# Fusing the stages of a transducer joint's forward and backward pass into one stream of 512-column chunks

## The chip, the cores and the metric

The kernel runs on one core of a Trainium2 chip. The metric is device time of that core in microseconds (us): the median of several runs of one kernel. The profiles are taken from one of those runs, so a span in a profile differs a little from a median.

Engines in the profile: PE is the matmul engine (TensorE), PEld its weight loads, DVE is VectorE, ACT is ScalarE, POOL is GpSimd, SP is SyncE. "PEclk" is the granted clock of TensorE as a share of full speed. In these kernels PSUM is where matmuls leave their sums, SBUF where the other tiles lie, and DRAM holds inputs, outputs and spills (data stored and loaded again later). Some traces lack matmul records (7790 matmuls for 7868 weight loads in the kernel before), so PE's busy time is probably a few us too small.

## The reference

Two convolutions of width 3 and stride 2 with a tanh-approximated gelu, then a joint of every time step with every one of 8 labels, then the gradients of all seven inputs. With B=2, T=16000, D=V=256 the joint has 4000 time steps per batch. The core of it:

```python
h = einsum over 3 taps of x with w1;   h = gelu(h)[:, ::2, :]     # (2, 8000, 256)
f = einsum over 3 taps of h with w2;   f = gelu(f)[:, ::2, :]     # (2, 4000, 256)
fe = f @ w_f;   ge = g @ w_g                                      # g: (2, 8, 256)
j = tanh(fe[:, :, None, :] + ge[:, None, :, :])                   # (2, 4000, 8, 256)
out = j @ w_o
_out, _vjp = jax.vjp(_f, x, w1, w2, g, w_f, w_g, w_o)
_grads = _vjp(grad_out)        # the outputs are out and the seven gradients
```

(The first five lines are shortened; the padding is left out.) Everything is bfloat16 in memory, with FP32 sums.

## The kernel before

Each batch passes through five stages, one after the other. Each stage has its own buffers, above all its own PSUM pools, which are freed before the next begins. A batch has 8 chunks of 512 columns (a column is a time step; the last chunk has 416), and every stage goes over all of them.

1. Conv: both convolutions and their gelu. The gelu derivatives and a row-major copy of h go to DRAM.
2. Joint: tanh, outputs, the gradient through tanh, the sum of it over the labels, the gradient of w_o.
3. GF/GH: gradients back through w_f, gelu, w2, gelu.
4. W2/WF: weight gradients, with transposes on PE and copies of them.
5. x/W1: the gradient of x (tile GX_SB, stored straight to DRAM) and of w1.

The gelu, which sets the pace of the conv stage: four operations on VectorE and ScalarE lie between the matmuls and the release of their PSUM buffer, then five more make the derivative.

```python
def gelu_from_psum(wk, Pps, W, h_out, gp_out):
    sq = wk.tile([P, KT, CW], BF16, name="g_sq")
    nc.scalar.activation(out=sq[:, :, :W], in_=Pps, func=ACT.Square, scale=GELU_SQRT_K)
    inner = wk.tile([P, KT, CW], BF16, name="g_inner")
    nc.vector.scalar_tensor_tensor(out=inner[:, :, :W], in0=sq[:, :, :W], scalar=1.0, in1=Pps,
                                   op0=ALU.add, op1=ALU.mult)
    s = wk.tile([P, KT, CW], BF16, name="g_s")
    nc.scalar.activation(out=s[:, :, :W], in_=inner[:, :, :W], func=ACT.Sigmoid, scale=GELU_A)
    nc.vector.tensor_tensor(out=h_out, in0=s[:, :, :W], in1=Pps, op=ALU.mult)
    # ... five more operations for the derivative gp_out (one on ScalarE, four on VectorE)
```

The order of stages, and what is spilled between them:

```python
for b in range(B):
    # ... GE = g @ w_g
    with tc.tile_pool(name="psA", bufs=2, space=PSUM) as psA, ...:      # stage 1
        for ci in range(n_cchunks + 1):
            if ci < n_cchunks:
                conv1_chunk(ci, wk, g1p, psA)      # ends in a store of both derivatives to G1D
            if ci >= 1:
                conv2_chunk(ci - 1, wk, g2p, psB)  # ends in a store to G2D
                hrc_chunk(ci - 1, hrp, psHR)       # transposes of h, stored to HRD
    # ... stage 2, joint, over all chunks
    # ... stage 3: d1_chunk / d5_chunk, reload G2D and G1D
    # ... stage 4: reload HRD; per 256 columns:
            pe_transpose8(psD3t, FNg[:], srcs)     # 8 transposes and one copy of 1024 columns
            pe_transpose8(psD3t, GFR[:], srcs)
            # ... matmuls into GWF_ps and GW2_ps, which stay in PSUM for the whole batch
    # ... stage 5: GX_SB and GW1_ps, which stays in PSUM too
```

Of the kernel before, what the change touches and what calls it, by code (L numbers as in the profile page):

```python
# [10 lines left out]
BF16 = mybir.dt.bfloat16  # L11
# [10 lines left out]
def kernel(  # L22
# [31 lines left out]
    n_cchunks = (MQ + CW - 1) // CW  # L54
    MQ_PAD = n_cchunks * CW
    NBLK = MQ_PAD // 128
    CBLK = CW // 128
    HOFF = 16
    HW = HOFF + MQ_PAD + 16
    GFW = MQ_PAD + 128  # L60
    TBF = 512
    assert TBF <= CW and MQ_PAD % TBF == 0
    NTB = TBF // 128
    n_tb_total = MQ_PAD // 128
    n_jchunks = MQ_PAD // TBF

    const = ctx.enter_context(tc.tile_pool(name="const", bufs=1))
    accp = ctx.enter_context(tc.tile_pool(name="accp", bufs=1))
    dram = ctx.enter_context(tc.tile_pool(name="dscr", bufs=1, space=bass.MemoryType.DRAM))

    xcp = ctx.enter_context(tc.tile_pool(name="xc", bufs=3))
    xq = x.rearrange("b (q four) d -> b four q d", four=4)

    def load_xc(bb, ci):
        mc0 = ci * CW
        W = min(CW, MQ - mc0)
        XC = xcp.tile([P, 4, KT, CW + 16], BF16, name="XC")
        if ci == 0:
            nc.vector.memset(XC[:, :, :, 0:16], 0.0)
            q0, j0, n = 0, 16, W  # L80
        else:
            q0, j0, n = mc0 - 16, 0, W + 16
        for c in range(4):
            nc.sync.dma_start_transpose(out=XC[:, c, :, j0:j0 + n], in_=xq[bb, c, q0:q0 + n, :])
        return XC

    xc_prefetched = {(0, 0): load_xc(0, 0)}

    ident = const.tile([P, P], BF16, name="ident")
    make_identity(nc, ident[:])  # L90
    ones = const.tile([P, 8], BF16, name="ones")
    nc.vector.memset(ones[:], 1.0)
    biasA = const.tile([P, 1], FP32, name="biasA")
    nc.vector.memset(biasA[:], GELU_A)

    W1 = const.tile([P, KK, KT, D], BF16, name="W1")
    nc.sync.dma_start(out=W1[:], in_=w1.rearrange("i (kt p) n -> p i kt n", p=P))
    W2 = const.tile([P, KK, KT, D], BF16, name="W2")
    nc.sync.dma_start(out=W2[:], in_=w2.rearrange("i (kt p) n -> p i kt n", p=P))
    WF = const.tile([P, KT, D], BF16, name="WF")  # L100
    nc.sync.dma_start(out=WF[:], in_=w_f.rearrange("(kt p) n -> p kt n", p=P))
    WG = const.tile([P, KT, D], BF16, name="WG")
    nc.sync.dma_start(out=WG[:], in_=w_g.rearrange("(kt p) n -> p kt n", p=P))
    WO = const.tile([P, KT, V], BF16, name="WO")
    nc.sync.dma_start(out=WO[:], in_=w_o.rearrange("(kt p) n -> p kt n", p=P))
    W1T = const.tile([P, KK, KT, D], BF16, name="W1T")
    W2T = const.tile([P, KK, KT, D], BF16, name="W2T")
    WFT = const.tile([P, KT, D], BF16, name="WFT")
    WOT = const.tile([P, KT, D], BF16, name="WOT")
    WGT = const.tile([P, KT, D], BF16, name="WGT")  # L110

    def make_transposed_weights():
        jobs = []
        for i in range(KK):
            for ktp in range(KT):
                for dt in range(KT):
                    jobs.append((W1T[:, i, ktp, dt * P:(dt + 1) * P], W1[:, i, dt, ktp * P:(ktp + 1) * P]))
                    jobs.append((W2T[:, i, ktp, dt * P:(dt + 1) * P], W2[:, i, dt, ktp * P:(ktp + 1) * P]))
        for WT_, W_ in ((WFT, WF), (WOT, WO), (WGT, WG)):
            for ktp in range(KT):  # L120
                for dt in range(KT):
                    jobs.append((WT_[:, ktp, dt * P:(dt + 1) * P], W_[:, dt, ktp * P:(ktp + 1) * P]))
        with tc.tile_pool(name="wtps", bufs=2, space=bass.MemoryType.PSUM) as wtps:
            for j0 in range(0, len(jobs), 4):
                grp = jobs[j0:j0 + 4]
                ps = wtps.tile([P, 4, P], FP32, name="wt_ps")
                for j, (dst, src) in enumerate(grp):
                    nc.tensor.matmul(ps[:, j, :], lhsT=src, rhs=ident[:], start=True, stop=True)
                for j, (dst, src) in enumerate(grp):
                    if (j0 // 4 + j) % 2 == 0:  # L130
                        nc.scalar.copy(out=dst, in_=ps[:, j, :])
                    else:
                        nc.vector.tensor_copy(out=dst, in_=ps[:, j, :])
# [5 lines left out]
    NGGE_parts = accp.tile([P, B, KT, U, n_jchunks], FP32, name="NGGE_parts")  # L139
    n_blocks_v = (MQ + P - 1) // P  # L140
    psgwo = ctx.enter_context(tc.tile_pool(name="ps_gwo", bufs=1, space=bass.MemoryType.PSUM))
    GWO_ps = psgwo.tile([P, KT, V], FP32, name="GWO_ps")
    gwo_cnt = [0]
    GR8 = accp.tile([U, B, D], BF16, name="GR8")
    for b in range(B):
        nc.sync.dma_start(out=GR8[:, b, :], in_=g[b])

    HRD = dram.tile([P, NBLK, 2, KT, P], BF16, name="HRD")
    G1D = dram.tile([2, P, KT, MQ_PAD], BF16, name="G1D")
    G2D = dram.tile([P, KT, MQ_PAD], BF16, name="G2D")  # L150

    tr_ctr = [0]

    def pe_transpose8(ps_pool, dst_ap, srcs, eng=None):
        ps = ps_pool.tile([P, 8, P], BF16, name="tr8_ps")
        for j, src in enumerate(srcs):
            nc.tensor.transpose(out=ps[:, j, :], in_=src, identity=ident[:])  # L157
        if eng is None:
            eng = "act" if tr_ctr[0] % 2 == 0 else "dve"
            tr_ctr[0] += 1  # L160
        if eng == "act":
            nc.scalar.copy(out=dst_ap, in_=ps[:])  # L162
        else:
            nc.vector.tensor_copy(out=dst_ap, in_=ps[:])  # L164

    def gelu_from_psum(wk, Pps, W, h_out, gp_out):
        sq = wk.tile([P, KT, CW], BF16, name="g_sq")
        nc.scalar.activation(out=sq[:, :, :W], in_=Pps, func=ACT.Square, scale=GELU_SQRT_K)
        inner = wk.tile([P, KT, CW], BF16, name="g_inner")
        nc.vector.scalar_tensor_tensor(out=inner[:, :, :W], in0=sq[:, :, :W], scalar=1.0, in1=Pps,  # L170
                                       op0=ALU.add, op1=ALU.mult)
        s = wk.tile([P, KT, CW], BF16, name="g_s")
        nc.scalar.activation(out=s[:, :, :W], in_=inner[:, :, :W], func=ACT.Sigmoid, scale=GELU_A)
        nc.vector.tensor_tensor(out=h_out, in0=s[:, :, :W], in1=Pps, op=ALU.mult)  # L174
        oms = wk.tile([P, KT, CW], BF16, name="g_oms")
        nc.scalar.activation(out=oms[:, :, :W], in_=s[:, :, :W], func=ACT.Identity,
                             scale=-GELU_A, bias=biasA[:])
        rr = wk.tile([P, KT, CW], BF16, name="g_rr")
        nc.vector.tensor_scalar(out=rr[:, :, :W], in0=sq[:, :, :W], scalar1=3.0, scalar2=1.0,
                                op0=ALU.mult, op1=ALU.add)  # L180
        nc.vector.tensor_tensor(out=rr[:, :, :W], in0=oms[:, :, :W], in1=rr[:, :, :W], op=ALU.mult)  # L181
        nc.vector.tensor_tensor(out=oms[:, :, :W], in0=rr[:, :, :W], in1=h_out, op=ALU.mult)  # L182
        nc.vector.tensor_tensor(out=gp_out, in0=oms[:, :, :W], in1=s[:, :, :W], op=ALU.add)

    for b in range(B):
        bctx = ExitStack()
        bpers = bctx.enter_context(tc.tile_pool(name="bpers", bufs=1))
        FT = bpers.tile([P, KT, MQ_PAD], BF16, name="FT")
        NGFE_T = bpers.tile([P, KT, MQ_PAD], BF16, name="NGFE_T")
        GE = bpers.tile([P, KT, U], FP32, name="GE")  # L190
        if MQ < MQ_PAD:
            nc.gpsimd.memset(FT[:, :, MQ:MQ_PAD], 0.0)

        with tc.tile_pool(name="ge_sb", bufs=1) as gsb, tc.tile_pool(name="ge_ps", bufs=1, space=bass.MemoryType.PSUM) as gps:
            gT_ps = gps.tile([P, KT, U], BF16, name="gT_ps")
            for kt in range(KT):
                nc.tensor.transpose(out=gT_ps[:, kt, :], in_=GR8[:, b, kt * P:(kt + 1) * P],
                                    identity=ident[:U, :U])
            gT = gsb.tile([P, KT, U], BF16, name="gT")
            nc.vector.tensor_copy(out=gT[:], in_=gT_ps[:])  # L200
            ge_ps = gps.tile([P, KT, U], FP32, name="ge_ps")
            for mt in range(KT):
                for kt in range(KT):
                    nc.tensor.matmul(ge_ps[:, mt, :], lhsT=WG[:, kt, mt * P:(mt + 1) * P], rhs=gT[:, kt, :],
                                     start=(kt == 0), stop=(kt == KT - 1))
            nc.vector.tensor_copy(out=GE[:], in_=ge_ps[:])

# [479 lines left out]
```

## Time and profile before

The median was 1118.37 us in 3 runs (1113.61 to 1130.01).

| What | Value |
|---|---|
| span of the profiled run | 1113.3 us |
| PE busy | 966.8 us, so idle for 146.5 us |
| VectorE, ScalarE busy | 728.1, 550.6 us |
| DMA | 197.65 MB |
| clock granted to TensorE, mean | 0.961 |

The first part of the page of the kernel before (busy time, share of the span, number of instructions), and its line of DMA packets:

```profile
span 1113.3 us, 19863 instructions
PE 966.8 (87%) x7790; PEld 689.8 (62%) x7868; DVE 728.1 (65%) x1476; ACT 550.6 (49%) x831; POOL 188.0 (17%) x346
...
DMA packets 254590, 197.65 MB, mean 178 GB/s; under 512 B 206400, under 2 KB 223328, under 8 KB 254496
```

An average of 87% hides very different stages. The view by windows of the kernel before gives each stage of batch 0 a row. The columns are the stretch in us from the span's start, its length, the busy time of each engine with the number of instructions, the clock, the busy share of the DMA engines, and GB/s:

```profile
core 0: us, PE busy (x) PEld busy (x) DVE busy (x) ACT busy (x) POOL busy (x), PEclk, DMA share, GB/s
19.00:140.00 121.00, 81.73 (x436) 41.32 (x443) 109.07 (x163) 91.47 (x108) 21.70 (x34) 0.87 0.66 167
140.00:375.00 235.00, 229.64 (x1912) 168.34 (x1938) 184.60 (x464) 140.32 (x256) 34.89 (x65) 0.98 0.87 208
375.00:407.00 32.00, 29.45 (x136) 13.28 (x139) 29.49 (x49) 0.00 (x0) 0.94 (x3) 1.00 0.76 251
407.00:465.00 58.00, 45.63 (x520) 39.72 (x519) 13.06 (x21) 16.19 (x16) 5.33 (x11) 1.00 0.28 92
465.00:560.00 95.00, 93.41 (x890) 81.64 (x891) 29.01 (x45) 26.05 (x40) 30.45 (x56) 1.00 0.50 167
```

In the conv stage (first row) PE works 81.7 of 121 us, while VectorE works 109; in the joint (second row) and the x/W1 gradients (last row) PE is 98% busy and VectorE has room. The W2/WF stage (fourth row) leaves 12 us of PE unused and VectorE at 23%. The groups of instructions of the kernel before show what that stage waits for (after the bar: busy us and mean ns, then the idle time of the engine just before them, and its releaser):

```profile
L162 ACT COPY FNg<-tr_ps 128x1024 bf16<-128x1024 bf16 x32 | 32.4, 1012 | 142.5 <-PE tr_ps L157 142.5
...
L537 PE MATMUL GWF_ps<-FNg 128*128 128x256 bf16 x128 | 24.8, 275 | 22.0 <-ACT FNg L162 22.0
```

PE waited 22.0 us, over both batches, for copies of transposes on ScalarE, which in that stage of batch 0 is itself only 16.19 of 58 us busy.

### The profile page before, as it was taken

What the parts mean: (1) busy time and instruction counts of PE and PEld (TensorE: products, weight loads), DVE (VectorE), ACT (ScalarE), POOL (GpSimd) and SP (SyncE); (2) the same over time, 40 slices, a digit from 0 to 9 for tenths busy, and PEclk for the clock granted to TensorE, in tenths of its full rate; (3) what the DMA queues carried; (4) which work ended last, traced back from release to release, by engine and by line L of the source; (5) the groups of instructions that cost most, each with busy time, mean ns of one, the idle gap of its engine ahead of it and who ended that gap; (6) DMA issues with size and microseconds to landing.
All of it is one profiled execution on the core that took longest, in us unless ns stands there. A gap on an engine that the chain in (4) does not pass through costs nothing.

```text
span 1113.3 us, 19863 instructions
## 1 busy us (share of the span) xinstructions
PE 966.8 (87%) x7790; PEld 689.8 (62%) x7868; DVE 728.1 (65%) x1476; ACT 550.6 (49%) x831; POOL 188.0 (17%) x346
## 2 busy tenths in 40 slices
PE   3876589999999987799987765999999999779995
PEld 1433257777777556688843332777777774668884
DVE  2999768888888761323279994788888879223322
ACT  2788585555664112222358877555555530222233
POOL 0112111111111110033212121111111110103330
PEclk9999689999999999999999986999999999999997
DMA  8767499889894572066357428988898737414552
GB/s 190 179 167 184 133 210 270 227 171 252 181 252 160 190 241 85 32 196 210 124 109 201 127 108 176 246 214 223 213 209 233 208 110 263 152 39 148 203 175 89
DMA packets 254590, 197.65 MB, mean 178 GB/s; under 512 B 206400, under 2 KB 223328, under 8 KB 254496
## 3 DMA queue, kind: packets, MB, share of 16 engines
q1 hardware_dynamic: 220192, 72.99, 32.9%
q0 software_dynamic: 34304, 123.39, 32.6%
q8 instruction: 61, 1.00, 0.4%
q14 instruction: 33, 0.27, 0.1%
HBM read 75.41 MB, written 71.31 MB: 132 GB/s over the span
## 4 chain that ended last, share of the span: by engine, by line
PE 65%; DVE 12%; ACT 4%; issue 3%; DMA 3%; SPq 1%; ACTq 0%; POOL 0%; DVEq 0%; POOLq 0%
PE O_ps L351 10%; PE GWO_ps L367 10%; PE gj_ps L402 9%; PE psE_t L585 8%; PE sum_ps L393 5%; PE jr_ps L342 5%; ACT FNg L162 3%; PE tr_ps L157 3%; PE GWF_ps L537 2%; DVE g_inner L170 2%; DVE g_rr L181 1%; DVE GH_To L476 1%; DVE GF_T L453 1%; DVE GH_Te L467 1%; DVE g_oms L182 1%
## 5 line engine op out<-in xcount | busy, mean ns | idle before, releaser
L354 ACT CAST OUT_SB<-O_ps 128x512 bf16<-128x512 f32 (+1 forms) x256 | 139.3, 602 | 196.3 <-PE O_ps L351 96.5
L407 DVE SCALAR_TENSOR_TENSOR NGZ<-JSQ,gj_ps 128x512 bf16<-128x512 bf16 (+1 forms) x256 | 172.5, 674 | 87.6 <-PE gj_ps L402 68.8
L321 ACT ACTIVATE JT<-gj_ps,GE 128x512 bf16<-128x512 f32 (+1 forms) x256 | 155.2, 719 | 2.4 <-remote 1.5
L402 PE MATMUL gj_ps<-GOT,WOT 128*128 128x512 bf16 (+1 forms) x469 | 142.5, 378 | 8.8 <-DMA GOT<-in_grad_out_dram 5.9
L351 PE MATMUL O_ps<-WO,JT 128*128 128x256 bf16 (+1 forms) x1024 | 137.7, 276 | 3.1 <-ACT JT L321 3.1
L367 PE MATMUL GWO_ps<-GO_R,JR 128*128 128x256 bf16 (+1 forms) x1024 | 134.4, 274 | 0.3 <-issue 0.2
L591 DVE CAST GX_SB<-psE_t 128x512 bf16<-128x512 f32 x64 | 44.2, 691 | 132.0 <-PE psE_t L585 54.6
L237 PE MATMUL psA_t<-XC,W_81 128*128 128x512 bf16 (+1 forms) x377 | 97.5, 412 | 36.9 <-DVE HTo L174 19.2
L367 PEld LDWEIGHTS <-JR 128*128 128x128 bf16 (+1 forms) x1024 | 100.0, 98 | 38.8 <-issue 1.9
L405 DVE TENSOR_TENSOR JSQ<-JT 128x512 bf16<-128x512 bf16 (+1 forms) x256 | 105.6, 414 | 14.8 <-ACT JT L321 2.4
L351 PEld LDWEIGHTS <-JT 128*128 128x128 bf16 (+1 forms) x1024 | 95.9, 99 | 15.1 <-ACT JT L321 4.0
L162 ACT COPY FNg<-tr_ps 128x1024 bf16<-128x1024 bf16 x32 | 32.4, 1012 | 142.5 <-PE tr_ps L157 142.5
L589 ACT CAST GX_SB<-psE_t 128x512 bf16<-128x512 f32 x64 | 37.6, 587 | 129.6 <-PE psE_t L585 106.5
L393 PE MATMUL sum_ps<-NGZ,ident 128*128 128x512 bf16 (+1 forms) x254 | 93.1, 377 | 2.2
L237 PEld LDWEIGHTS <-W_81 128*128 128x128 bf16 x384 | 40.0, 105 | 85.5 <-issue 44.2
L342 PEld LDWEIGHTS <-JT 128*128 128x128 bf16 (+1 forms) x1024 | 68.9, 99 | 38.4 <-ACT JT L321 8.1
L345 DVE COPY JR<-jr_ps 128x1024 bf16<-128x1024 bf16 (+1 forms) x128 | 88.3, 690 | 2.5 <-DMA GO_R<-in_grad_out_dram 1.9
L342 PE MATMUL jr_ps<-ident,JT 128*128 128x128 bf16 (+1 forms) x1024 | 81.4, 221 | 5.5 <-ACT JT L321 3.0
L585 PE MATMUL psE_t<-W1T,GH_Te 128*128 128x256 bf16 (+1 forms) x384 | 75.6, 273 | 3.8 <-DVE ACC_GW_97 L547 1.9
L164 DVE COPY GFR<-tr_ps 128x1024 bf16<-128x1024 bf16 x32 | 22.1, 692 | 84.0 <-PE tr_ps L157 84.0
L585 PE MATMUL psE_t<-W1T,GH_To 128*128 128x256 bf16 (+1 forms) x384 | 73.3, 273 | 0.0
L333 POOL DMA_DIRECT2D GO_R<-in_grad_out_dram x64 | 34.5, 540 | 227.8 <-PE GWO_ps L367 219.4
(754 smaller groups left out, 1696.9 us busy)
## 6 DMA issues: line engine op xcount, KB each, us to landing
GO_R<-in_grad_out_dram POOLq DMA_DIRECT2D x62, 512.0 KB, 4.5
out_dram<-OUT_SB POOLq DMA_DIRECT2D x62, 512.0 KB, 4.3
out_dram<-GX_SB POOLq DMA_DIRECT2D x62, 256.0 KB, 2.6
G1D<-G1c_w POOLq DMA_DIRECT2D x32, 256.0 KB, 2.7
HRD<-HRc POOLq DMA_DIRECT2D x16, 512.0 KB, 3.2
G1c<-G1D SPq DMA_DIRECT2D x32, 256.0 KB, 4.4
HRg<-HRD SPq DMA_DIRECT2D x16, 512.0 KB, 4.9
G2D<-G2c_w POOLq DMA_DIRECT2D x16, 256.0 KB, 2.7
```

What stands on the lines that cost most here:

```text
L237: nc.tensor.matmul(ps[:, mt, :W], lhsT=W1[:, i, kt, mt * P:(mt + 1) * P], rhs=XC[:, c, kt, j:j + W], start=(k == 0), stop=(k == nmm - 1))
L321: nc.scalar.activation(out=JT[:, mt, u, :W], in_=FE_ps[:, :W], func=ACT.Tanh, bias=GE[:, mt, u:u + 1], scale=1.0)
L342: nc.tensor.transpose(out=tr[:Mv, j, kt, :], in_=JT[:, kt, hf * UH + j, tb * P:tb * P + Mv], identity=ident[:])
L345: nc.vector.tensor_copy(out=JR[:Mv], in_=tr[:Mv])
L351: nc.tensor.matmul(O_ps[:Mv, jj, :], lhsT=JT[:, kt, u, tb * P:tb * P + Mv], rhs=WO[:, kt, :], start=(kt == 0), stop=(kt == KT - 1))
L354: nc.scalar.copy(out=OUT_SB[:Mv, u0:u0 + 2, :], in_=O_ps[:Mv])
L367: nc.tensor.matmul(GWO_ps[:, dt, :], lhsT=JR[:Mv, j, dt, :], rhs=GO_R[:Mv, hf * UH + j, :], start=(n == 0), stop=(n == n_gwo_total - 1))
L393: nc.tensor.matmul(sum_ps[dt][:, :W], lhsT=ident[:], rhs=NGZ[:, :W], start=(u == 0), stop=(u == U - 1))
L402: nc.tensor.matmul(gj_ps[:, :W], lhsT=WOT[:, kt, dt * P:(dt + 1) * P], rhs=GOT[:, kt, u, :W], start=(kt == 0), stop=(kt == KT - 1))
L405: nc.vector.tensor_tensor(out=JSQ[:, :W], in0=JT[:, dt, u, :W], in1=JT[:, dt, u, :W], op=ALU.mult)
L407: nc.vector.scalar_tensor_tensor(out=NGZ[:, :W], in0=JSQ[:, :W], scalar=1.0, in1=gj_ps[:, :W], op0=ALU.subtract, op1=ALU.mult, accum_out=N ...
L585: nc.tensor.matmul(ps[:Mq, cj, :], lhsT=SRC[:, kt, q0 + sh:q0 + sh + Mq], rhs=W1T[:, i, kt, :], start=(k == 0), stop=(k == nmm - 1))
```

## The change: its intent, and the diff

The Trainium skill, "Perfetto Trace Analysis", section "Optimization Strategy" under "Identifying Performance Opportunities", describes this situation: where the most contended engine changes over time, "performance may be improved by interleaving those regimes". The change does that. There is now one list of 16 chunks (8 of each batch). One turn of the loop runs the joint of chunk k, the conv of chunk k+1 and all gradients of chunk k-1, with their instructions written alternately. What the conv makes stays in SBUF until the gradients have used it, so nothing is spilled. The core of the diff (the bodies of the stages, rewritten as generators, are cut):

```diff
-    dram = ctx.enter_context(tc.tile_pool(name="dscr", bufs=1, space=bass.MemoryType.DRAM))
+    keep = ctx.enter_context(tc.tile_pool(name="keep", bufs=3))
+    gxp = ctx.enter_context(tc.tile_pool(name="gxp", bufs=2))
+    psG = ctx.enter_context(tc.tile_pool(name="psG", bufs=1, space=bass.MemoryType.PSUM))
+    psS = ctx.enter_context(tc.tile_pool(name="psS", bufs=1, space=bass.MemoryType.PSUM))
+    psJ = ctx.enter_context(tc.tile_pool(name="psJ", bufs=3, space=bass.MemoryType.PSUM))
+    psA = ctx.enter_context(tc.tile_pool(name="psA", bufs=2, space=bass.MemoryType.PSUM))
...
-        if b == 0:
-            make_transposed_weights()
+    make_ge()
+    gen = stage_a(0)
+    for up in range(2):
+        st[0].setdefault("GOT", {})[up] = load_got(0, up)
+        st[0].setdefault("GO", {})[up] = load_gor(0, up)
+    nc.sync.dma_start_transpose(out=WOT[:], in_=w_o[:, :])
+    for _ in gen:
+        pass
...
+    for k in range(NG + 1):
+        gj_ = stage_j(k) if k < NG else None
+        ga = stage_a(k + 1) if k + 1 < NG else None
+        gd = stage_de(k - 1) if k >= 1 else None
+        na, nd = [0], [0]
+        for step in range(NSTEP):
+            if gj_ is not None:
+                next(gj_)
+            ga = advance(ga, na, step + 1)
+            gd = advance(gd, nd, max(0, step - 1) * NDE // (NSTEP - 2))
```

Some things must change with it. The joint has a PSUM pool of three buffers, and the conv and the gradients share one of two (psA). The weight gradients cannot stay in PSUM; each chunk adds seven sums to FP32 accumulators in SBUF (`acc_add`, on VectorE). One gelu operation moves from ScalarE to VectorE. Outputs and grad_out move by pairs of labels, in rows of 1 KB instead of 4 KB. The transposed weights come by DMA transposes. The order in which the program writes instructions is a priority and not the order of execution.

## The prediction

> **What bounds the kernel now.** The page gives PE 966.8 us busy of 1113.3 (87%), DVE 728.1, ACT 550.6. Windows by stage (batch 0 / batch 1):
> - Joint, 235 / 224 us: PE 229.6 / 222.4 busy, DVE 184.6 / 177.5. PE-bound, nothing to win.
> - Conv, 121 / 108 us: PE only 81.7 / 78.4, DVE 109 / 100. DVE-bound, with a reduced clock (0.87 and 0.94).
> - GF/GH gradients, 32 / 30 us: PE and DVE both about 93%.
> - W2/WF gradients, 58 / 58 us: PE 45.6; the chain alternates with 1.02 us ACT copies of transposes (FNg) while DVE is 23% busy.
> - x/W1 gradients, 95 / 94 us: PE 98%.
> - Start 19, batch joint 25 and end 14 us are nearly empty of PE work.
>
> So about 146 us of the span have no matmul, and conv runs partly at the low clock. A PE that never waits needs, per 512-column chunk, 28.5 (joint) + 11.9 + 5.8 + 3.6 + 8.7 (conv at full clock: 40 passes of 512 columns at the 0.216 us spacing seen) = 58.5 us; over 15.6 chunks about 914 us.
>
> **What the change does.** Removed: all DRAM spills (G1D, G2D, HRD and their reloads, about 42 MB of 198 MB), the matmul-made transposed weights, stage boundaries, the batch joint. These were mostly not on the chain; the gain is filling PE's idle time in conv and in the W2 gradients with joint matmuls.
> Added on DVE per chunk: seven PSUM-to-accumulator adds (0.69 us each; before only per batch), FE evacuations (2 x 0.69), the gelu's 1-s term moved from ACT (1.13 us) to DVE (about 0.41 us, as the other tensor_scalar), halves of 512 instead of 1024 columns. Saved: 16 JSQ of 0.41 become 8 of 0.67. From the stage windows DVE becomes about 51 us per chunk (ACT about 35). DVE is then nearly as full as PE (87% of it).
> PSUM: joint work has three buffers, everything else two. A gelu half holds one for matmul 1.3 + Square 0.57 + 0.67 + Sigmoid 0.6 + 0.67 us plus queue waits. My estimate of all holding times is about 100 us per chunk for two buffers, 50 us each, so this too is close to the limit.
> DMA: 37 us of 16-engine time per chunk from the present shares (transposes 40%, copies 44% in the joint stage), a little more for 1 KB rows instead of 4 KB; no bound.
> Tables: Sigmoid and Tanh now alternate. The Trainium skill, "ScalarE: Activation LUTs", section "Table sets", puts both in one set; the trace agrees (two table loads of 1283 ns in all). No thrash.
> Clock: the skill's "TensorE: Matmul & The Clock Gate", Part 1, says PE idleness halves the clock; the trace shows 0.87 in the first conv stage against 1.00 in the gradient stages. A single stream should stay near 1.0.
>
> **Sum.** PE efficiency in the steady stream: an estimate of 0.91 (joint alone had 0.99, the GF/GH stage 0.93, but PE, DVE and two PSUM buffers are now all near full). 914/0.91 = 1004, plus about 27 us before the joint starts (conv of chunk 0 alone), 9 us in the last gradients, 12 us final stores: 1052 us.
>
> **Right if** PE is about 93% of a shorter span with clock 0.98 or more; DVE is above 75%; steady chunks take 62 to 66 us; PE's remaining waits are on DVE ops that release the two-buffer pool (g_s products, ACC adds); DMA bytes fall by about a fifth; two table loads.
> **Wrong if** the gelu chains and the two buffers serialize with joint work (chunks above 69 us: no gain or slower), 1 KB rows make GOT/GO late, or the order of instructions blocks DVE behind Sigmoid. Better if PE reaches 97%.
>
> Chances: faster 0.78, same 0.14, slower 0.08.

## The result, and the profile after

The kernel after took 1051.54 us (4 runs, 1049.27 to 1056.34). Its ratio to the kernel before is 0.9401 with a 95% interval of 0.9317 to 0.9485. A ratio here is the mean time of one kernel's fast runs over that of the other's of the same rounds, so it is not quite the ratio of the medians quoted. Executions over 1.5% slower than the fastest of the same kernel are left out of the means.

The first part of the page of the kernel after, and its DMA packets:

```profile
span 1051.0 us, 19369 instructions
PE 966.0 (92%) x7718; PEld 677.9 (64%) x7832; DVE 800.6 (76%) x1612; ACT 517.7 (49%) x869; POOL 199.1 (19%) x372
...
DMA packets 237210, 156.50 MB, mean 149 GB/s; under 512 B 208352, under 2 KB 212992, under 8 KB 237120
```

PE's busy time is the same (966.8 and 966.0 us). What shrank is its idle time, from 146.5 to 85.0 us, and that is nearly the whole of the gain (61.5 of 62.3 us). VectorE has 72.5 us more work, and DMA moves 21% fewer bytes.

The view by windows of the kernel after shows the start, the first turn of the loop, two turns in the middle, the end, and a long stretch of the middle (a turn begins here where the first gradient matmul of a chunk begins):

```profile
core 0: us, PE busy (x) PEld busy (x) DVE busy (x) ACT busy (x) POOL busy (x), PEclk, DMA share, GB/s
0.00:52.10 52.10, 17.51 (x61) 6.85 (x63) 16.03 (x32) 10.39 (x16) 7.21 (x21) 0.91 0.80 179
52.10:103.80 51.70, 49.17 (x372) 31.93 (x376) 48.26 (x101) 41.06 (x71) 6.56 (x10) 0.99 0.63 149
166.00:227.00 61.00, 59.12 (x483) 42.57 (x490) 50.47 (x101) 32.17 (x54) 11.51 (x21) 1.00 0.69 171
227.00:288.00 61.00, 58.51 (x480) 42.25 (x487) 49.89 (x99) 31.72 (x53) 11.50 (x21) 1.00 0.64 146
1006.50:1051.00 44.50, 27.72 (x197) 15.55 (x196) 12.87 (x24) 12.28 (x20) 3.90 (x8) 0.87 0.18 57
225.00:345.00 120.00, 114.97 (x946) 83.23 (x958) 97.81 (x195) 62.26 (x104) 22.24 (x41) 1.00 0.65 153
```

A full chunk of the stream takes about 61.0 us. VectorE's 50 us and ScalarE's 32 us per chunk are close to the predicted 51 and 35. In the first 52.1 us little more than the conv of chunk 0 is done.

How much PE work is in these windows can be counted from the code, in units of 512 columns: 128 for the joint of a full chunk, 46 for its conv stage, 90 for its gradients, together 264. At the pace of 0.216 us that the trace shows for 512 columns, that is 57.0 us. In the window of the first turn the trace's own records add up to 208 units, the joint of chunk 0, the conv of chunk 1 and the first matmuls of the chunks that follow; with two missing records that makes 210 units, or 45.4 us, while the window reports 49.17 busy. The Trainium skill, "Trainium Kernel Development and Optimization", in its note on reading a trace, calls matmul busy time "a bad metric" for how close a kernel is to its limit, because matmuls are pipelined. This trace agrees, by a small amount: 49.17 us of "busy" for an estimated 45.4 us of columns.

A chunk of 416 columns is less of a saving than it looks. Its last block has 32 or 33 time steps instead of 128, but the trace shows matmuls of 256 columns for it too. Counted from the code, such a chunk is 244.5 units (119 joint, 38.5 conv, 87 gradients) and not 264 x 416/512 = 214.5. All 16 chunks are then 4185 units, or 15.85 full chunks.

The table of waits of the kernel after gives what PE waited for (total us, times, longest):

```profile
PE psa L468 <- ACT GX_SB L175: 16.6, 11, 3.4
PE psab L157 <- DMA GR_137<-in_g_dram: 15.1, 1, 15.1
PE psa L164 <- DMA g_sq<-in_w_g_dram: 6.8, 1, 6.8
PE psj L329 <- DMA WOT<-in_w_o_dram: 4.7, 1, 4.7
PE psa L499 <- ACT GX_SB L175: 3.5, 3, 1.7
```

The same view for ScalarE and for VectorE:

```profile
ACT GX_SB L175 <- DMA out_dram<-GX_SB: 60.7, 20, 6.1
...
DVE GX_SB L177 <- DMA out_dram<-GX_SB: 20.2, 12, 3.5
```

Three of PE's five largest waits belong to the start and occur once. The other two have one cause. PE waits for ScalarE to copy a piece of the gradient of x from PSUM to the tile GX_SB, and ScalarE waits, for 60.7 us in all, until an earlier store of GX_SB has landed, because that tile has only two buffers (the experiment with a third one below tests this). Line L468 is the weight-gradient matmul, which needs a PSUM buffer (psa) that an uncopied GX piece still holds.

One such wait, in the timeline of ScalarE of the kernel after (start, us, then in brackets the idle time before it and its releaser):

```profile
265.11 0.58 ACT L175 CAST OUT_SB<-psj 128x512 bf16<-128x512 f32 x1 [0.21 <-PE psj L365]
269.99 0.58 ACT L175 CAST GX_SB<-psa 128x512 bf16<-128x512 f32 x1 [4.30 <-DMA out_dram<-GX_SB]
270.47 0.59 ACT L175 CAST OUT_SB<-psj 128x512 bf16<-128x512 f32 x1
```

And what PE does at that time, in its timeline:

```profile
270.63 0.27 PE L468 MATMUL psa<-GHoR,X_2692 128*128 128x256 bf16 x1 [1.63 <-ACT GX_SB L175]
```

ScalarE stands for 4.30 us; PE stands for 1.63 us, until that copy is made. The view of tile GX_SB gives the time from the issue of such a store to its landing:

```profile
DMA to landing us min/median/max: 1.6/3.0/7.8
```

The Trainium skill, "DMA: Bandwidth & Descriptors", section "Anatomy of one DMA", gives about 2.0 us of fixed cost plus bytes over 436 GB/s; for these 256 KB that makes 2.6 us, as an estimate of its formula. The trace's median of 3.0 is near it, but in this busy stream one store can take 7.8 us, and with two buffers it is the late ones that count.

The stall seems to have a second cost. The granted clock of TensorE was 0.50 for 6.8 us from 575.3 us, just after a wait on GX_SB of 1.75 us, and again for 6.8 us from 885.9 us, during one of 3.45 us; in these stretches matmuls of 256 columns start about 0.21 us apart, where 0.11 is usual. With the third buffer below, no such stretch lies between the first turn and the end.

### The profile page after: what moved, and what is told of

Its sections match the earlier page's. It is cut to its first block, busy times and chain, and to the rows that moved or that the text cites. A ratio compares the mean times of both kernels' runs of the same rounds, so it can differ in the third digit from the quotient of the medians.

```text
span 1051.0 us, 19369 instructions
## 1 busy us (share of the span) xinstructions
PE 966.0 (92%) x7718; PEld 677.9 (64%) x7832; DVE 800.6 (76%) x1612; ACT 517.7 (49%) x869; POOL 199.1 (19%) x372
## 4 chain that ended last, share of the span: by engine, by line
PE 69%; DVE 11%; DMA 9%; ACT 5%; issue 4%; SPq 2%; POOL 0%; another core or an unknown queue 0%; ACTq 0%; POOLq 0%
PE psa L468 14%; PE psa L215 11%; PE psj L365 8%; DMA out_dram<-GX_SB 8%; PE GWO_ps L293 8%; PE psj L329 7%; PE psa L499 5%; PE psjb L349 4%; PE psab L184 3%; PE psa L442 3%; SPq L98 2%; PE psa L431 1%; ACT JT L280 1%; ACT g_sq L195 1%; DVE g_s L196 1%
## 5 line engine op out<-in xcount | busy, mean ns | idle before, releaser
L175 ACT CAST OUT_SB<-psj 128x512 bf16<-128x512 f32 (+1 forms) x256 | 149.7, 585 | 202.6 <-PE psj L365 183.2
L335 DVE SCALAR_TENSOR_TENSOR NGZ<-JSQ,psj 128x512 bf16<-128x512 bf16 (+1 forms) x256 | 170.5, 670 | 49.5 <-PE psj L329 43.2
L365 PE MATMUL psj<-WO,JT 128*128 128x256 bf16 (+1 forms) x1024 | 161.7, 273 | 1.0 <-DVE NGZ L335 0.5
L329 PE MATMUL psj<-GOT,WOT 128*128 128x512 bf16 (+1 forms) x457 | 139.6, 376 | 6.1 <-DMA WOT<-in_w_o_dram 4.7
L215 PE MATMUL psa<-XC,W_116 128*128 128x512 bf16 (+1 forms) x362 | 92.5, 386 | 4.7 <-DVE HTo L198 3.1
L177 DVE COPY JR<-psjb 128x1024 bf16<-128x1024 bf16 (+2 forms) x136 | 88.4, 654 | 2.1 <-PE psjb L349 1.4
L333 DVE TENSOR_TENSOR JSQ<-JT 128x1024 bf16<-128x1024 bf16 (+1 forms) x128 | 86.2, 675 | 2.2
L349 PE MATMUL psjb<-ident,JT 128*128 128x128 bf16 (+1 forms) x1024 | 86.4, 221 | 0.5 <-issue 0.3
L175 ACT CAST GX_SB<-psa 128x512 bf16<-128x512 f32 x64 | 37.3, 582 | 83.3 <-DMA out_dram<-GX_SB 60.7
L499 PE MATMUL psa<-W1T,GHo 128*128 128x256 bf16 (+1 forms) x384 | 73.2, 272 | 4.1 <-ACT GX_SB L175 3.5
L499 PE MATMUL psa<-W1T,GHe 128*128 128x256 bf16 (+1 forms) x384 | 73.3, 272 | 0.2
```

The source lines that it names most:

```text
L175: nc.scalar.copy(out=out, in_=in_)
L177: nc.vector.tensor_copy(out=out, in_=in_)
L215: nc.tensor.matmul(ps[:, :W], lhsT=w[:, mt * P:(mt + 1) * P], rhs=rhs, start=(k == 0), stop=(k == len(mms) - 1))
L329: nc.tensor.matmul(gj[:, :W], lhsT=WOT[:, kt, dt * P:(dt + 1) * P], rhs=GOT[:, j, kt, :W], start=(kt == 0), stop=(kt == KT - 1))
L333: nc.vector.tensor_tensor(out=JSQ[:, :, :W], in0=JT[:, j, :, :W], in1=JT[:, j, :, :W], op=ALU.mult)
L335: nc.vector.scalar_tensor_tensor(out=NGZ[:, :W], in0=JSQ[:, dt, :W], scalar=1.0, in1=gj[:, :W], op0=ALU.subtract, op1=ALU.mult, accum_out= ...
```

## The experiments

Every kernel below gave correct results. The runs on two chips each had the kernel before beside them: 1116.19 us (median of 7, on the chip of the first four) and 1119.56 us (median of 7; 1116.49 for the five fast ones, on the chip of the last four). On the second chip the formal verdicts are "unclear"; the record gives no reason, but two of the seven runs of the kernel before were slow. The intervals of the ratios are given. Where kernels of the two chips are compared, I take the difference of their ratios times about 1117 us.

The theory: the stream's pace is set by PE, with a stall on top from the two GX_SB buffers; the rest of the loss is at the two ends; the lower DRAM traffic is worth nothing by itself. The rivals: the shared pool of two PSUM buffers or VectorE limits the stream (this is what the prediction held), or the gain came from the removed spills.

### Control: the kernel after again

> The changed kernel itself, unaltered, as the control of this series. Both theories: 1051 us, within 4 us, ratio to the kernel before 0.94.

Measured: 1048.02 us (1045.76 to 1049.58), ratio 0.938 (0.9317 to 0.9444). The stall is there again; the waits of this run:

```profile
ACT GX_SB L175 <- DMA out_dram<-GX_SB: 57.5, 18, 5.5
```

### A third buffer for GX_SB

```diff
-    gxp = ctx.enter_context(tc.tile_pool(name="gxp", bufs=2))
+    gxp = ctx.enter_context(tc.tile_pool(name="gxp", bufs=3))
```

> One more buffer for the x-gradient block GX (3 instead of 2), nothing else. Theory A (the steady stream is held by PE; what PE still waits for per chunk is the eviction of GX, which itself waits for the store of GX two blocks earlier; the trace has 60.7 us of ACT and 20.2 us of DVE waits on that store and 20 us of PE waits behind them): 1030 to 1040 us, and these waits fall to a few us. Rival B (the stream is held by VectorE and the two PSUM buffers for everything but the joint work, so the freed time is lost to the next wait): within 4 us of the control.

Measured: 1023.0 us (1021.52 to 1024.2), ratio 0.9161 (0.911 to 0.9213), so 25 us less than the control and 7 us below the range that was expected. ScalarE's line of waits in this run:

```profile
ACT GX_SB L175 <- DMA out_dram<-GX_SB: 3.0, 2, 1.5
```

And the long stretch of the middle in its view by windows (columns as above):

```profile
225.00:345.00 120.00, 118.29 (x968) 85.42 (x983) 101.34 (x200) 64.18 (x106) 23.69 (x43) 1.00 0.67 160
```

The wait fell from 57.5 to 3.0 us. In the same 120 us, PE is now busy for 118.29 us where the kernel after had 114.97, and a full chunk takes 59.56 us instead of 61.0. The stores themselves did not get faster (median 3.4 us, longest 8.2): the third buffer hides them. This shows that the stall in the middle of the stream came from the two output buffers. The gain is more than PE's 21.0 us of waits on GX_SB in the control: over the profiled span PE's idle time fell by 20.9 us (84.8 to 63.9) and its busy time by 4.2 (962.7 to 958.5). Part of the latter is the clock: the control had one stretch of 3.4 us at 0.50 in the stream, this run none. The page "Perfetto Trace Analysis" of the Trainium skill, in "Optimization Strategy", describes such a case as "Consistent bubbles": the same gap repeating on the engine that should be saturated can come from a lack of buffers.

The chain of waits that ended last puts 8% of the span of the kernel after, about 84 us, on these stores. Removing them gave 25 us. A share of that chain is not yet a gain.

### The label projection after the first conv

The start of the kernel after, in PE's timeline:

```profile
15.15 0.21 PE L157 MATMUL psab<-ident,GR_137 8*128 8x8 bf16 x2 [15.15 <-DMA GR_137<-in_g_dram]
22.20 0.27 PE L164 MATMUL psa<-gT_156,g_sq 128*128 128x8 bf16 x4 [6.84 <-DMA g_sq<-in_w_g_dram]
...
27.29 0.61 PE L329 MATMUL psj<-GOT,WOT 128*128 128x512 bf16 x1 [4.68 <-DMA WOT<-in_w_o_dram]
...
27.84 5.08 PE L215 MATMUL psa<-XC,W_116 128*128 128x512 bf16 x12
...
36.27 4.29 PE L215 MATMUL psa<-XC,W_116 128*128 128x512 bf16 x12 [3.13 <-DVE HTo L198]
```

In the kernel before, the first conv matmul started at 13.90 us; here it starts at 27.84. Ahead of it in PE's queue stand the tiny matmuls of the label projection, which wait for g and w_g, and a joint matmul, which waits for the transposed w_o. The Trainium skill, "TensorE: Matmul & The Clock Gate", Part 2, "Step-by-step: what each phase is for", says that matmuls stay in program order and that only weight loads are pulled ahead; the trace agrees, as no conv matmul overtakes these 0.2 to 0.6 us instructions during 12.7 us (15.15 to 27.84), though its inputs land at about 14.3 us in the next run. A second thing can be seen here: the two groups of 12 conv matmuls take 5.08 and 4.29 us, or about 0.42 and 0.36 us each, where 512 columns take 0.216 later. Part 1 of that page says that an idle TensorE runs at half clock. The trace agrees for the second group, whose granted clock was 0.63; for the first the view gives 1.00, but the trace's clock records begin only at 32.6 us, so it can't tell.

```diff
-    make_ge()
     gen = stage_a(0)
@@
     for _ in gen:
         pass
+    make_ge()
```

> The small matmuls for g (they wait for g and then w_g, until 22.4 us) emitted after the conv of chunk 0 instead of before it. Theory A (the start is an in-order queue on PE: the first conv matmul stood at 27.8 us behind matmuls that waited for g, w_g and the transposed w_o): first conv matmul at about 15 us, total 7 to 13 us below the control. Rival B (the start is set by the loads of x, grad_out and the transposed weights): first joint matmuls stay at about 52 us, total within 4 us of the control.

Measured: 1040.6 us (1038.34 to 1042.03), ratio 0.9318 (0.9265 to 0.9371), so 7.4 us less than the control. PE's timeline of this run:

```profile
14.34 4.31 PE L215 MATMUL psa<-XC,W 128*128 128x512 bf16 x12 [14.34 <-DMA XC<-in_x_dram]
21.93 1.04 PE L329 MATMUL psj<-GOT,WOT 128*128 128x512 bf16 x2 [3.28 <-DMA WOT<-in_w_o_dram]
22.76 5.24 PE L215 MATMUL psa<-XC,W 128*128 128x512 bf16 x12
```

The first conv matmuls now start at 14.34 us, 13.5 us earlier, and so does the second group (22.76 instead of 36.27), although it still stands behind the joint matmul that waits for w_o. What takes back part of the 13.5 us is the other end of the move: the tanh of the joint needs the label projection, which now stands behind the conv's transposes, so the first tanh starts at 43.40 us, just after the projection's last step, where it started at 51.30 in the kernel after. So the blocking at the head of the queue is shown to cost at least these 7.4 us.

### The spills put back

The five tiles that the conv keeps for the gradients are stored to DRAM and loaded again one turn later; the interleaving stays as it is. (One tile's lines.)

```diff
-        G2 = keep.tile([P, KT, CW], BF16, name="G2")
+        G2 = keep.tile([P, KT, CW], BF16, name="G2", bufs=2)
@@ end of the conv stage
+        for n_ in ("G1e", "G1o", "G2", "HRo", "HRe"):
+            for sl in spill_parts(n_, g_):
+                nc.gpsimd.dma_start(out=SPILL[n_][g_][sl], in_=S[n_][sl])
@@ last part of the joint of the same chunk
+                for sl in spill_parts(n_, g_):
+                    nc.sync.dma_start(out=S[n_ + "_r"][sl], in_=SPILL[n_][g_][sl])
```

> The DRAM round trip put back into the one-stream kernel: both conv gelu derivatives, the second one's, and the two row forms of h are stored to DRAM at the end of their stage and reloaded a chunk later before the gradients use them, about 42 MB in all as in the kernel before. Theory A (the gain is PE idle time filled by overlap; the DMA engines had room): within 8 us of the control. Rival B (a good part of the gain is the removed traffic): 20 to 60 us slower than the control.

Measured: 1044.53 us (1042.65 to 1049.38), ratio 0.9361 (0.9305 to 0.9418), against 1048.02 for the control: no loss. Its DMA packets:

```profile
DMA packets 261269, 197.52 MB, mean 189 GB/s; under 512 B 211040, under 2 KB 228248, under 8 KB 261176
```

It moves as many bytes as the kernel before (197.65 MB) and keeps the whole gain. So in the fused stream 41 MB of saved traffic is not what made the kernel faster. The words "nothing spilled" in the change describe something that came with the gain but did not cause it.

### More work on TensorE

```diff
                 gj = ps_j()
+                nc.tensor.matmul(gj[:, :W], lhsT=WOT[:, 0, dt * P:(dt + 1) * P], rhs=GOT[:, j, 0, :W],
+                                 start=True, stop=True)
                 for kt in range(KT):
```

The real pair of matmuls overwrites the extra one, so the result stays correct. It adds 256 matmuls of up to 512 columns.

> 256 extra 512-column matmuls (16 per chunk, each overwritten by the grad_out matmul that follows it, so the result stays right), at the 0.216 us spacing of the trace about 54 us of TensorE work; about 5% more. Theory A (the stream is bound by TensorE): 44 to 56 us slower than the control (1048 us), that is 1092 to 1104. Rival B (VectorE or the PSUM buffers bind, TensorE has room): less than 20 us slower.

Measured: 1081.26 us (1079.05 to 1083.02), ratio 0.9656 (0.96 to 0.9711). Against the control that is 0.0276 of 1117 us, or 31 us, for about 54 us of added PE work (224 matmuls of 512 columns at 0.216 us and 32 of 416 at 0.176). The first part of the control's page, then of this run's:

```profile
PE 962.7 (92%) x7718; PEld 676.7 (65%) x7832; DVE 800.3 (76%) x1612; ACT 517.8 (49%) x869; POOL 199.2 (19%) x372
...
PE 1013.1 (94%) x8088; PEld 699.3 (65%) x8088; DVE 805.7 (75%) x1612; ACT 518.1 (48%) x869; POOL 199.8 (18%) x372
```

Its waits at GX_SB, of ScalarE and then of PE:

```profile
ACT GX_SB L175 <- DMA out_dram<-GX_SB: 47.8, 16, 5.5
...
PE psa L470 <- ACT GX_SB L175: 13.9, 10, 2.4
```

The outcome lies between the ranges of both theories: 1 us of PE work cost about 0.6 us. Part of the rest is the GX_SB stall, which has more time to end: ScalarE's wait fell from 57.5 to 47.8 us, and PE's waits on GX_SB from 21.0 to 15.5. PE's busy time can't give the balance: it grew by 50.4 us, but 114 matmul records are missing from the control's trace (7718 of 7832) and none from this run's. The length of the turns can. Two full turns of this run have no wait on GX_SB and take 62.44 and 62.45 us; a turn without that wait takes 59.56 us in the last kernel of this section, on the same chip. So without the stall 16 added matmuls (3.46 us at 0.216 each) cost 2.9 us a turn, about 0.8 of their time, and the stall hid much of the rest. Why not the full time is not settled.

### More work on VectorE

```diff
-                    nc.vector.tensor_tensor(out=JSQ[:, :, :W], in0=JT[:, j, :, :W], in1=JT[:, j, :, :W], op=ALU.mult)
+                    for _ in range(2):
+                        nc.vector.tensor_tensor(out=JSQ[:, :, :W], in0=JT[:, j, :, :W], in1=JT[:, j, :, :W], op=ALU.mult)
```

> Every JSQ square computed twice: 128 extra VectorE instructions of 0.67 us, about 79 us of VectorE time or 10% more; VectorE would be 84% busy. Theory A: VectorE has room, 0 to 20 us slower than the control. Rival B (VectorE co-limits, since it already does 51 of 61 us per chunk): 50 us slower or more.

Measured: 1066.67 us (1062.88 to 1068.49), ratio 0.9526 (0.9479 to 0.9574). By ratios that is 0.0146 of 1117 us, or 16 us more than the control. VectorE's busy time grew by 70.0 us, from 800.3 to 870.3, so 1 us of it cost about 0.23 us. Most of that can be seen in PE's waits for a PSUM buffer that VectorE copies out into the tile FE (the product f @ w_f): 13.0 us in this run against 3.1 in the control. VectorE is not the main bound, but it isn't free either.

### Two buffers for the joint and three for the rest

Done on top of the third GX_SB buffer:

```diff
-    psJ = ctx.enter_context(tc.tile_pool(name="psJ", bufs=3, space=bass.MemoryType.PSUM))
-    psA = ctx.enter_context(tc.tile_pool(name="psA", bufs=2, space=bass.MemoryType.PSUM))
+    psJ = ctx.enter_context(tc.tile_pool(name="psJ", bufs=2, space=bass.MemoryType.PSUM))
+    psA = ctx.enter_context(tc.tile_pool(name="psA", bufs=3, space=bass.MemoryType.PSUM))
```

> On top of gx3 (1023 us): one PSUM buffer moved from the joint work to everything else (2 and 3 instead of 3 and 2). The prediction said that the two buffers are close to a limit (100 us of holding time per chunk for two). If so: 10 to 25 us faster than gx3. If the scheduled order hides those holding times, as the few waits in the trace suggest: within 5 us of gx3, or slower because the joint work has one buffer less.

Measured: 1036.54 us (1036.04 to 1036.96), ratio 0.9261 (0.9222 to 0.93), against 0.9161 with the pools as they were: about 11 us slower. PE's waits in this run show why:

```profile
PE psj L365 <- DVE NGZ L335: 8.7, 14, 1.4
...
PE psj L365 <- ACT OUT_SB L175: 4.5, 11, 0.4
```

PE now waits for the joint's pool (psj). The prediction had named the pool of two as a limit. Had it been one, a third buffer there should have shown a gain; moving the buffer cost time instead. The total does not separate what the third buffer gave from what the joint lost, but the kernel with three GX_SB buffers and two psA buffers has PE busy for 118.29 of 120 us, which leaves nearly nothing for that pool to cost in the stream. At the ends it does seem to cost something: the two traces, of different chips, put the first gradient matmul at 101.1 us with three psA buffers and 103.7 with two, and the last turn at 39.1 and 43.3 us. The stream between went from 875.4 to 894.0 us, which is where the joint lost.

### A version that beats both

The third GX_SB buffer, the label projection after the first conv, the transposed w_o ahead of the grad_out loads, and the last stores in another order, on rotating buffers:

```diff
-    gxp = ctx.enter_context(tc.tile_pool(name="gxp", bufs=2))
+    gxp = ctx.enter_context(tc.tile_pool(name="gxp", bufs=3))
@@
-    make_ge()
     gen = stage_a(0)
+    nc.sync.dma_start_transpose(out=WOT[:], in_=w_o[:, :])
@@
-    nc.sync.dma_start_transpose(out=WOT[:], in_=w_o[:, :])
     for _ in gen:
         pass
+    make_ge()
@@
-            t_full = gel.tile([P, KT, CW], BF16, name="g_sq")
+            nm = ("g_sq", "g_s", "g_om")[n_store[0] % 3]
+            n_store[0] += 1
+            t_full = gel.tile([P, KT, CW], BF16, name=nm, **({"bufs": 1} if nm == "g_om" else {}))
@@
         store(out_7, GWO_ps[:])
+        store(out_5, ACC_GWF[:], -1.0)
+        for i in range(KK):
+            store(out_3[i], ACC_GW2[:, i])
```

> gx3 and ge_late together, the transposed w_o loaded ahead of grad_out at the start, and the final stores emitted in the order in which their sums are ready, on four to five buffers instead of two. If the parts add up: 1048 - 25 - 7 for the first two, 2 to 4 for w_o (conv waited 3.3 us for it) and 6 to 8 for the stores: 1004 to 1010 us.

Measured: 1011.98 us (1010.6 to 1015.48), ratio 0.9047 (0.9002 to 0.9092): 9.5% less than the kernel before, 2 us above the expected range. PE's timeline at the start of this run:

```profile
14.74 1.01 PE L215 MATMUL psa<-XC,W 128*128 128x512 bf16 x2 [14.74 <-DMA XC<-in_x_dram]
16.00 4.42 PE L215 MATMUL psa<-XC,W 128*128 128x512 bf16 x10 [0.25 <-DMA XC<-in_x_dram]
20.22 0.85 PE L329 MATMUL psj<-GOT,WOT 128*128 128x512 bf16 x2
23.77 4.44 PE L215 MATMUL psa<-XC,W 128*128 128x512 bf16 x12 [2.71 <-DVE HTo L198]
```

No wait for weights is left there: PE waits for x, and then for VectorE's gelu. The first gradient matmul starts at 95.3 us (103.6 in the control), and the last gradients and stores take 37.9 us after their first matmul (44.5 in the kernel after). A chunk takes 59.56 us, as with the third GX_SB buffer alone.

### Not run

Four more kernels: the additions on PE and on VectorE again on top of the third GX_SB buffer, the stages written one after another within a turn of the loop, and the kernel before with three instead of two buffers for its transposes of stage 4. So three things stay open: whether PE work costs its full time once the GX_SB stall is gone (the two turns above say about 0.8 of it); how much of the gain needs the alternate writing of instructions, beyond the overlap that the chunked stream allows; and how much of the W2/WF stage's idle time a buffer alone would have recovered in the kernel before.

## Why the prediction was right or wrong

The predicted time was 1052 us and the measured one 1051.54. The close agreement is partly luck: the stream was predicted about 37 us too long and the ends about 36 us too short. The measured column uses the profiled span of 1051.0 us. The work at the ends is taken at the stream's pace of 61.0 us for 264 units, as an estimate (10.0 us for the 43 units recorded before 52.1 us, 48.5 for the 210 of the first turn of the loop, 20.1 for the 87 of the last chunk's gradients).

| Term | predicted us | measured us |
|---|---|---|
| a full chunk in the stream | 58.5 / 0.91 = 64.3 | 61.0 |
| all chunks (predicted as 15.625 full ones, counted as 15.85) | 1004 | 967 |
| before the joint starts, beyond the conv's own work | 27 | 52.1 - 10.0 = 42.1 |
| first turn of the loop, beyond its work | 0 | 51.7 - 48.5 = 3.2 |
| turn at the batch boundary, beyond 61.0 | 0 | 69.7 - 61.0 = 8.7 |
| last gradients and stores, beyond the work | 9 + 12 = 21 | 44.5 - 20.1 = 24.4 |
| other turns (the remainder) | 0 | 5.6 |
| sum | 1052 | 1051 |

Point by point:

- **What bounds the kernel before: right as far as the traces go.** Nearly the whole gain of 62 us in the profiled spans is idle time of PE (146.5 to 85.0 us) at the same busy time. The stages with PE idle are gone: between the ends, PE is busy for 115 of 120 us. The overlap itself was not undone in any run; what speaks for it is this idle time, and that the spills, put back, cost nothing.
- **"Mostly not on the chain" for the spills: right, and shown.** With the spills back the kernel takes 1044.53 us, no more than the control.
- **"An estimate of 0.91": wrong.** 58.5/61.0 makes 0.96, and 0.98 with the third GX_SB buffer (58.5/59.56). The reason given for 0.91 was that PE, VectorE and two PSUM buffers would all be nearly full. VectorE was about as full as predicted, but adding 70 us to it cost only 16 us, which suggests that its fullness is worth little. Chunks took 61.0 us, just below the predicted 62 to 66.
- **"Two PSUM buffers close to the limit", and "PE's remaining waits are on DVE ops that release the two-buffer pool": wrong.** With two buffers PE can be busy for 118.29 of 120 us. An estimated holding time that nearly fills two buffers did not make PE wait in the stream. PE's remaining waits were indeed for a buffer of that pool, but what held it was a GX piece, until ScalarE copied it into GX_SB, and behind that copy a store's landing: 20.1 us, where the prediction named VectorE's gelu products and sums. The failed step is that the prediction checked DMA only for bandwidth ("no bound") and never for the latency of one store against the number of its buffers; that was worth 25 us.
- **"About 27 us before the joint starts" and "9 us in the last gradients, 12 us final stores": too small.** The start alone costs 42.1 us, in part because the order of PE's queue puts matmuls with late inputs ahead of the conv; taking the label projection out of the way gave back 7.4 us. The turn at the batch boundary was not in the sum at all; the 6.8 us at a granted clock of 0.50 and a GX_SB wait lie in it, and with the third buffer it is 64.94 instead of 69.75 us. Together the last five terms cost 84 us and not 48. In the other direction, the chunks of 416 columns were counted as 0.8125 of a full one, which hid about 14 us of the error in the 0.91.
- **The checks:** PE at 92% of the span (predicted about 93), mean clock 0.983 (0.98 or more), VectorE at 76% (above 75), DMA bytes down by 21% (about a fifth): all as predicted. Sigmoid and Tanh in one table set as well, as the page cited in the prediction says: the groups of instructions of the kernel after show no reload of tables in 16 turns:

```profile
L195 ACT ACT_TABLE_LOAD x1 | 1.3, 1283 | 18.7 <-DMA GR_137<-in_g_dram 18.7
L197 ACT ACT_TABLE_LOAD x1 | 1.3, 1283 | 0.0
```

One reservation remains on the first point. That PE is the main bound of the stream is supported by its busy share and by 0.6 us of cost for 1 us of added work, against 0.23 for VectorE; the missing 0.4 is partly the GX_SB stall (0.8 in the turns without it), and the rest stays open.

## What to carry to other kernels

When stages with different limits are fused into one stream, estimate the stream from the busiest engine's work, then look for its remaining stall in the buffers of outputs: here two buffers left ScalarE 57.5 us of waits although the median store landed in 3.1 us, so look at the late stores and not at the median. Budget the ends of the stream apart, since little overlaps there, count partial chunks by their matmuls and not by their columns, and keep instructions with late inputs from the head of an in-order queue. A total that comes out right proves none of its terms; check each term against the profile.

## What the Trainium skill lacked or had wrong

- "DMA: Bandwidth & Descriptors", "Anatomy of one DMA": the fit gives an estimated 2.6 us for the 256 KB stores of the gradient of x. The median in the stream was 3.0 us, and the longest 7.8. The page warns that a write's completion can take surprisingly long, but gives no figure for how far a single store can lag in a busy stream, which matters for the number of buffers: the third one was worth 25 us here (1048.02 to 1023.0).
- "Perfetto Trace Analysis", "Optimization Strategy": it recommends interleaving regimes, which this confirms (ratio 0.9401), and names bubbles from too few buffers, which it confirms too. It doesn't say that the stream's two ends then hold most of what is left: by the estimates above about 42 us at the start and 24 us at the end of 1051.0.
- "TensorE: Matmul & The Clock Gate", Part 2: matmuls in program order agrees with the trace. The page does not give the consequence for the start of a kernel, where matmuls of 0.2 to 0.6 us with late inputs kept the conv from starting until 27.84 us, against 14.34 once the label projection was moved.
- "Trainium Kernel Development and Optimization", note on reading a trace: agrees, by a small amount (49.17 us busy for an estimated 45.4 us of columns). Still, PE's busy time was the same in both kernels (966.8 and 966.0 us), and its idle time measured the gain well.
- No page that I drew on says that a share of the chain of waits is not a gain: the stores of GX_SB held 8% of it (about 84 us), and removing the wait gave 25 us.
